# A long convolution and soft-MoE kernel: high rows' product ahead of the folds and the low rows' product in odd steps, once the last stage runs

## The chip, the cores and the metric

The kernel runs on one core of one Trainium2 chip. The metric is the time of the program on the device in microseconds; lower is better. TensorE (PE) multiplies, with its weight loads listed apart as PEld; VectorE (DVE), ScalarE (ACT) and GpSimd (POOL) compute on vectors; SyncE (SP) issues nearly all DMAs here, in one queue, in order. Each engine works through its own instructions in order and waits for the others by semaphores.

## What is computed

A long causal convolution of each of 8 sequences of 5696 tokens by 128 channels with one filter, by Fourier transform, and then a soft mixture of experts over all 45568 tokens:

```python
Xf = np.fft.rfft(x, n=L, axis=1)          # L = 2 * S
Hf = np.fft.rfft(h, n=L, axis=0)
y = np.fft.irfft(Xf * Hf[None], n=L, axis=1)[:, :S, :]
...
logits = x @ phi                          # x: y as (45568, 128); 32 slots
d = softmax of logits over all tokens     # by column
slot_input = d.T @ x
slot_out[e] = np.maximum(slot_input[e] @ w1[e], 0) @ w2[e]
c = softmax of logits over the slots      # by row
out = c @ slot_out
```

All is float32.

## The kernel before

**The transform.** The length is split into 90 x 64, so each transform is a chain of small products with a change of layout between them, for which the data goes through DRAM. Four stages follow each other, in a pipeline over *steps* t. One step brings in one tile of one sequence: 8 tiles (`NJ`) make a sequence, and the filter counts as one more sequence, ahead of the eight; so there are 72 steps (`NA`) with new input.

- *First stage*, steps 0 to 71. `load_x` (L184) brings tile t + 3 into one of three buffers `xc`, by two DMAs. `fold` (L201) adds and subtracts the two mirrored halves of a tile on GpSimd, one operation each (L206), into the four buffers `xf`, two for even tiles and two for odd ones. `first_stage` (L210) multiplies folds by the table `s1` (L217), evicts both results through ScalarE (L220) into one of four staging tiles `fst`, and stores them by SP into the DRAM tensor f of the sequence (L226). The product is made in two widths. `first_low(t)` makes rows 0 to 59 of the two folds of tile t, with weights of 128 x 64; `first_high(t)`, in odd steps alone, makes rows 60 to 89 of the four folds of tiles t - 1 and t at once, with weights of 128 x 32 side by side. Either fills two PSUM banks. Low stores two DMAs of 240 KB, high four of 120 KB.
- *Middle stage*, from step 9 on. `prefetch` loads tiles `gt` from f (L253), into four buffers. `stage_b1` (L258) multiplies them (L267, 64 x 64), VectorE applies the filter's spectrum (L285, L294). `stage_b2` (L298) multiplies back (L309, 64 x 64), ScalarE evicts (L315), and SP stores to the DRAM tensor z (L318). Odd steps have one such unit, even steps two; twelve make a sequence.
- *Last stage*, from step 27 on (`LAG_C`), over pairs of tiles. `load_pair` (L338) loads `zc` by five DMAs (L346) in even steps; there is one such buffer. `stage_c1` (L352) makes four products (L365, 128 x 64) in odd steps, in two halves, with `stage_c4` of an earlier pair between them. Its VectorE and GpSimd work gives the tokens (L370 to L384). `stage_c2` transposes (L393), `stage_c3` makes the logits (L402, 128 x 32, the last product of an even step), `stage_c4` and `stage_c5` transpose them (L431, L454), `softmax`, `dispatch` (L480) and `stage_c6` (L506) do the mixture's two softmaxes.
- After step 80 a tail without new input, and then the experts and the output.

**The order of work** is written by hand. Each step runs through a string of letters, and each letter calls one part; instructions reach every engine's queue in that order, and nothing reorders them but what an engine does itself. For odd steps it is `"xXYf1wb5s"`, for even ones `"zPxXfb26db3m"`: `x` loads a tile, `X` is `first_low`, `Y` is `first_high`, `f` folds tile t + 1, `1` is the two halves of c1 with c4 between, `w` the rest of c1's vector work, `b` a unit of the middle stage, `5` and `s` are c5 and softmax, `z` is `load_pair`, `P` is `prefetch`.

The folds of tile t + 1 go into the buffers of tile t - 1. These are read for the last time by `first_high(t)`, so in an odd step the folds wait for its products. PSUM gives the stages a ring of four banks (`bank`, L173): each use waits for the eviction of the one four uses before.

Of the kernel before, what the change touches and what calls it, by code (L numbers as in the profile page):

```python
# [12 lines left out]
AL = mybir.AluOpType  # L13
# [64 lines left out]
def kernel(  # L78
# [24 lines left out]
    nc = tc.nc  # L103
# [3 lines left out]
    E, _, F = moe_w1.shape  # L107
# [16 lines left out]
    QP = HP // 2  # L124
# [18 lines left out]
    NT = B * NQ  # L143
# [34 lines left out]
    xs = {}  # L178
    xf = [apool.tile([P, CH, D], F32, name=f"x{i}", tag=f"x{i}", bufs=1) for i in range(4)]
# [16 lines left out]
                out=t_[X0 + r.start:X0 + r.stop, :, :, :].rearrange("p s n d -> p s (n d)"), in_=v)  # L196
        xs[c] = t_

    folded = {}

    def fold(c, comp):  # L201
        if c not in xs:
            return
        t_ = xs.pop(c) if comp else xs[c]
        y_ = xf[c % 2 * 2 + comp]
        nc.gpsimd.tensor_tensor(out=y_[:, :, :], in0=t_[:, 0, :, :], in1=t_[:, 1, ::-1, :],  # L206
                                op=AL.subtract if comp else AL.add)
        folded[(c, comp)] = y_

    def first_stage(tiles, width):  # L210

        st = apool.tile([P, CH, 2, D], F32, name="fst", tag="fst", bufs=4)
        for G in range(2):
            p = bank()
            for o, (c, comp) in enumerate(tiles):
                k = slice(0, HP) if width == HP else slice(HP, HP + QP)
                nc.tensor.matmul(p[o * width:(o + 1) * width, :], s1[:, comp + G, k],  # L217
                                 folded[(c, comp)][:, :, :].rearrange("p n d -> p (n d)"),
                                 start=True, stop=True)
            nc.scalar.activation(st[:, :, G, :],  # L220
                                 p[:, :].rearrange("p (n d) -> p n d", d=D), AF.Copy)
        for o, (c, comp) in enumerate(tiles):
            g, j = divmod(c, NJ)
            n0 = comp * HALF + CH * j
            k0, n = (0, N1A) if width == HP else (N1A, N1 - N1A)
            nc.sync.dma_start(  # L226
                out=fd[g].rearrange("q a r c d -> (q a) (r c d)")[k0:k0 + n, n0 * 2 * D:(n0 + CH) * 2 * D],
                in_=st[o * width:o * width + n, :, :, :].rearrange("k n c d -> k (n c d)"))
# [2 lines left out]
        first_stage([(c, comp) for comp in range(2)], HP)  # L231

    def first_high(c):

        both = [(c - 1 + i, comp) for i in range(2) for comp in range(2)]
        first_stage(both, QP)
        for b_ in both:
            del folded[b_]

    gs, prods = {}, {}  # L240

# [82 lines left out]
    zs, ys, Ls, ds = {}, {}, {}, {}  # L324
# [5 lines left out]
    om, op = [ypool.tile([P, CH, D], F32, name=n) for n in ("om", "op")]  # L330
# [18 lines left out]
                                    a=2)[r:r + n, j * w_:(j + 1) * w_])  # L349
        zs[T] = t_  # L350

    def stage_c1(T, between):  # L352
        t_ = zs.pop(T)
        kr = used if t_ is zn else P
        y_ = ybufs.pop(0)
        ybufs.append(y_)

        def part(v, f):
            k = (2 * v + f) * CH
            return y_[:, k:k + CH, 0:D] if f == 0 else y_[:, k + CH - 1:k - 1:-1, 0:D]  # L360

        def product(o, tab, q):
            p = bank()
            for h_ in range(2):
                nc.tensor.matmul(p[h_ * HP:(h_ + 1) * HP, :], i1[0:kr, tab, :],  # L365
                                 t_[0:kr, h_, o, :, q, :], start=True, stop=True)
            return p[:, :].rearrange("p (n d) -> p n d", d=D)

        def fold_out(even, minus, plus):
            nc.vector.tensor_tensor(out=plus, in0=even, in1=minus, op=AL.add)  # L370
            nc.vector.tensor_tensor(out=minus, in0=even, in1=minus, op=AL.subtract)

        b_, a_ = product(0, 1, 1), product(0, 0, 0)
        nc.scalar.activation(part(0, 0), b_, AF.Copy)
        fold_out(a_, part(0, 0), part(1, 0))
        between()
        b_, a_ = product(1, 1, 0), product(1, 2, 1)
        nc.scalar.activation(om[:, :, :], b_, AF.Copy)

        def after():  # L380
            fold_out(a_, om[:, :, :], op[:, :, :])
            for v, o_, eng in ((1, op, nc.gpsimd), (0, om, nc.vector if tail else nc.gpsimd)):
                for part_, sign in ((part(v, 1), AL.subtract), (part(v, 0), AL.add)):
                    eng.tensor_tensor(out=part_, in0=part(v, 0), in1=o_[:, :, :], op=sign)  # L384

        ys[T] = y_
        return after

    def stage_c2(T):
        for k in (3, 1, 0, 2) if tail else (3, 2, 1, 0):  # L390
# [149 lines left out]
    LAG_B, LAG_C = NJ + 1, 3 * NJ + 3  # L540
# [24 lines left out]
    for comp in range(2):  # L565
        fold(0, comp)
    wait_b2 = []
    ORDER_E, ORDER_O, XAHEAD = "xXYf1wb5s", "zPxXfb26db3m", 3

    for t in range(last_front + 1):  # L570
        us = list(units(t))

        def pair(lag):
            T, half = divmod(t - LAG_C - lag, 2)
            return T if half == 0 and 0 <= T < NT else None

        def prefetch(last):
            nonlocal loaded
            while loaded < len(queue) and queue[loaded][1] <= last:
                load_g(queue[loaded][0])  # L580
                loaded += 1

        def slot_b():
            fresh = bool(us)
            if fresh:
                u = us.pop(0)
                stage_b1(u, t < LAG_C or t >= NA)
                wait_b2.append(u)
            if len(wait_b2) > fresh:
                stage_b2(wait_b2.pop(0))  # L590

        T, U = pair(0), pair(2)
        after = []
        work_ = {
            "z": lambda: load_pair(pair(-1)) if pair(-1) is not None else None,
            "x": lambda: load_x(t + XAHEAD) if t < NA else None,
            "p": lambda: prefetch(t + 1) if t % NJ else None,
            "P": lambda: prefetch(t + 2),
            "q": lambda: prefetch(t + 1),
            "X": lambda: first_low(t) if t < NA else None,  # L600
            "Y": lambda: first_high(t) if t < NA and t % 2 else None,
            "f": lambda: [fold(t + 1, comp) for comp in range(2)] if t < NA else None,
            "d": lambda: dispatch(pair(3)) if pair(3) is not None else None,
            "b": lambda: slot_b(),
            "1": lambda: after.append(stage_c1(T, lambda: stage_c4(U) if U is not None else None))
            if T is not None else stage_c4(U) if U is not None else None,
            "w": lambda: [a_() for a_ in after],
            "2": lambda: stage_c2(pair(1)) if pair(1) is not None else None,
            "6": lambda: stage_c6(pair(5)) if pair(5) is not None else None,
            "5": lambda: stage_c5(U) if U is not None else None,  # L610
            "3": lambda: stage_c3(pair(1)) if pair(1) is not None else None,
            "m": lambda: column_max(pair(1)) if pair(1) is not None else None,
            "s": lambda: list(softmax(U)) if U is not None else None,
            "g": lambda: prefetch(t + 1) if t % NJ == 0 else None,
        }
        if t == last_front:
            if pair(-1) is not None:
                load_pair(pair(-1))
            assert T is None and U is None
            V = pair(1)  # L620
            assert (V - 2) % NQ == 0
            slot_b()
            stage_c2(V)
            slot_b()
            dispatch(V - 1)
            stage_c3(V)
            slot_b()
            column_max(V)
            assert not us and not wait_b2
            break  # L630
        for c_ in (ORDER_E if t % 2 else ORDER_O):
            work_[c_]()
        assert not us
        if t == NA:
            lead.close()
            wts = inner.enter_context(tc.tile_pool(name="wts", bufs=1, side="right"))
            w1s = wts.tile([P, E, F], F32, name="w1s")
        if NA < t <= NA + E:
            nc.sync.dma_start(out=w1s[:, t - NA - 1, :], in_=moe_w1[t - NA - 1])
# [3 lines left out]
    T = V + 1  # L643
# [18 lines left out]
    tail["pool"] = cload.enter_context(tc.tile_pool(name="cload", bufs=1))  # L662
    y_ = tail["pool"].tile([P, Q * CH, D + 1], F32, name="y2", tag="y2", bufs=1)

    after = stage_c1(T, lambda: stage_c4(V))
    after()
    stage_c5(V)
    list(softmax(V))
    nc.gpsimd.memset(y_[:, :, D:D + 1], 1.0)
# [6 lines left out]
    for V in range(T, NT):  # L676
# [8 lines left out]
        N = T + 1 if V == T else V + 2  # L685
        after = None
        if N < NT:
            after = stage_c1(N, lambda: stage_c4(V))
            load_pair(N + 2)
        else:  # L690
            stage_c4(V)
        if after:
            after()
        stage_c5(V)
        end = softmax(V)
        if V == NT - 1:
# [6 lines left out]
            list(end)  # L703
        if V == T:
            ybufs.insert(0, y_)
            stage_c1(T + 2, lambda: None)()
            load_pair(T + 4)
        else:
            for b in range(2 * (V - T - 1), min(2 * (V - T), B - 2)):
# [4 lines left out]
                    out=w2s[:, i:i + 2, :, :],  # L714
                    in_=moe_w2[i:i + 2].rearrange("e (p c) d -> p e c d", p=P))
    stage_c6(NT - 2)
    assert list(Ls) == [NT - 1] and not (ys or ds or prods or gs or zs or xs or folded or wait_b2)


    cload.close()  # L720
# [128 lines left out]
```

## Time and profile before

| | |
|---|---|
| Time, median of 3 runs | 864.3 us (862.36 to 867.85) |
| Time of the profiled execution | 866.8 us |
| Its span, first to last instruction | 864.8 us |
| TensorE clock granted, mean | 0.943 |
| DMA, mean over the span | 315 GB/s, 272.00 MB |
| Queue of SP, share of 16 DMA engines | 90.2% |

In the table of groups, a row names the line, the engine, the operation, what is written and read with its shape, and the count; then the busy time and the mean in ns of one; then the idle time of the engine just before these instructions, and what ended most of it. A row of the waits gives who waited for whom, the total in us, the number of times and the longest one. Steps 27 to 71, in which the order changes, lie between some 170 and 626 us of the span.

### The profile page before, as it was taken

How to read it: one execution, taken by the hardware profiler on the slowest of the kernel's cores; microseconds unless marked ns; L12 is line 12 of the kernel's file. 1: busy time of each engine (PE TensorE's matmuls, PEld its weight loads, DVE VectorE, ACT ScalarE, POOL GpSimd, SP SyncE). 2: the span in 40 equal slices, each digit the busy share in tenths (PEclk: the TensorE clock that was granted, in tenths of full speed). 3: DMA queues.
4: the chain of work that ended last, by engine and by line, in shares of the span. 5: the costliest groups of instructions: out<-in, count | busy, mean ns of one | idle time of the engine just before them, and what ended most of it. 6: DMA issues, size and time to landing. Idle time of an engine off the chain costs nothing.

```text
span 864.8 us, 20506 instructions
## 1 busy us (share of the span) xinstructions
PE 777.0 (90%) x7796; PEld 376.9 (44%) x7796; DVE 618.1 (71%) x929; ACT 437.7 (51%) x967; POOL 392.6 (45%) x372
## 2 busy tenths in 40 slices
PE   5888888788999999999999999999987888978882
PEld 1122333234444444444444444444444454445882
DVE  3058877666877878887888788777879886963542
ACT  2432344344656565665566566655644445562531
POOL 4453424245556556665566555556434332541000
PEclk9999999999999999999999999999999889997755
DMA  9888999999999999999999999999987887760998
GB/s 297 265 284 300 317 328 339 336 335 342 329 316 343 341 345 324 346 334 338 322 336 348 329 342 334 344 326 345 349 298 269 285 306 261 273 267 7 370 381 328
DMA packets 153244, 272.00 MB, mean 315 GB/s; under 512 B 11878, under 2 KB 110054, under 8 KB 150005
## 3 DMA queue, kind: packets, MB, share of 16 engines
q1 hardware_dynamic: 152571, 270.38, 90.2%
q8 instruction: 62, 1.02, 0.5%
q10 hardware_dynamic: 576, 0.31, 0.1%
q14 instruction: 35, 0.29, 0.1%
HBM read 142.57 MB, written 127.98 MB: 313 GB/s over the span
## 4 chain that ended last, share of the span: by engine, by line
PE 65%; DVE 13%; DMA 8%; issue 4%; POOL 2%; ACT 1%; SPq 1%; DVEq 0%; ACTq 0%; POOLq 0%
PE bank L217 17%; PE bank L365 13%; PE bank L309 8%; PE bt L267 8%; PE bank L393 6%; DMA out_dram<-o 5%; PE bank L480 3%; DVE p L285 3%; DVE bt L285 3%; DVE yf L294 3%; PE bank L402 2%; DMA zc<-z 2%; PE bank L431 2%; POOL x L206 1%; PE bank L454 1%
## 5 line engine op out<-in xcount | busy, mean ns | idle before, releaser
L206 POOL TENSOR_TENSOR x<-xc 128x512 f32<-128x512 f32 x144 | 180.1, 1274 | 229.6 <-PE bank L217 209.2
L217 PE MATMUL bank<-x,s 128*32 128x512 f32 (+1 forms) x1152 | 229.5, 611 | 17.5 <-POOL x L206 15.8
L315 ACT ACTIVATE zst<-bank 128x512 f32<-128x512 f32 (+1 forms) x184 | 98.6, 585 | 182.2 <-PE bank L309 166.7
L220 ACT ACTIVATE fst<-bank 128x512 f32<-128x512 f32 x216 | 127.5, 598 | 110.7 <-PE bank L217 95.9
L285 DVE TENSOR_TENSOR p<-bt,Hi 128x1024 f32<-128x1024 f32 x96 | 111.3, 1159 | 34.1 <-PE bt L267 33.3
L365 PE MATMUL bank<-zc,i 128*64 128x512 f32 x480 | 118.1, 614 | 8.5 <-DMA f<-fst 5.0
L217 PEld LDWEIGHTS bank<-x,s 128*32 128x32 f32 (+1 forms) x1152 | 55.9, 124 | 158.8 <-issue 74.9
L309 PE MATMUL bank<-yf,vt 64*64 64x256 f32 x1440 | 101.6, 389 | 26.0 <-DVE yf L294 25.8
L294 DVE TENSOR_TENSOR yf<-bt,p 128x512 f32<-128x512 f32 x192 | 119.3, 663 | 3.3
L267 PE MATMUL bt<-gt,wt 64*64 64x256 f32 x1620 | 113.5, 388 | 3.7 <-DMA gt<-f 2.8
L285 DVE TENSOR_TENSOR bt<-bt,Hr 128x1024 f32<-128x1024 f32 x96 | 113.0, 1177 | 0.0
L267 PEld LDWEIGHTS bt<-gt,wt 64*64 64x64 f32 x1620 | 54.0, 132 | 78.2 <-issue 35.3
L384 POOL TENSOR_TENSOR y<-y,op 128x512 f32<-128x512 f32 x64 | 77.9, 1217 | 9.8 <-DVE op L370 6.7
L309 PEld LDWEIGHTS bank<-yf,vt 64*64 64x64 f32 x1440 | 56.6, 135 | 57.0 <-issue 28.9
L370 DVE TENSOR_TENSOR y<-bank,y 128x512 f32<-128x512 f32 x32 | 22.1, 692 | 72.5 <-PE bank L365 69.5
L393 PE MATMUL bank<-ident,y 109*128 109x109 f32 x512 | 63.9, 276 | 1.3 <-DVE y L384 1.0
L384 POOL TENSOR_TENSOR y<-y,om 128x512 f32<-128x512 f32 x54 | 64.0, 1184 | 2.1
L365 PEld LDWEIGHTS bank<-zc,i 128*64 128x64 f32 x480 | 30.4, 137 | 71.9 <-issue 47.5
L393 PEld LDWEIGHTS bank<-ident,y 109*128 109x128 f32 x512 | 53.5, 149 | 17.8 <-issue 11.5
L395 ACT ACTIVATE yt<-bank 128x360 f32<-128x360 f32 x128 | 51.3, 492 | 3.2 <-PE bank L393 3.0
L802 PE MATMUL op<-so,cT 32*128 32x128 f32 x704 | 46.2, 380 | 5.5 <-ACT o L811 5.0
L285 DVE TENSOR_TENSOR p<-bt,turn 128x1024 f32<-128x1024 f32 (+1 forms) x12 | 14.2, 1179 | 47.5 <-PE bt L267 46.7
(95 smaller groups left out, 802.0 us busy)
## 6 DMA issues: line engine op xcount, KB each, us to landing
gt<-f SPq DMA_DIRECT2D x99, 512.0 KB
z<-zst SPq DMA_DIRECT2D x88, 512.0 KB
f<-fst SPq DMA_DIRECT2D x144, 240.0 KB
zc<-z SPq DMA_DIRECT2D x30, 1024.0 KB
xc<-in_x_dram SPq DMA_DIRECT2D x64, 320.0 KB
f<-fst SPq DMA_DIRECT2D x144, 120.0 KB
out_dram<-o SPq DMA_DIRECT2D x16, 1024.0 KB
zc<-z SPq DMA_DIRECT2D x90, 128.0 KB
```

Of the source, the lines that this page charges most:

```text
L206: nc.gpsimd.tensor_tensor(out=y_[:, :, :], in0=t_[:, 0, :, :], in1=t_[:, 1, ::-1, :], op=AL.subtract if comp else AL.add)
L217: nc.tensor.matmul(p[o * width:(o + 1) * width, :], s1[:, comp + G, k], folded[(c, comp)][:, :, :].rearrange("p n d -> p (n d)"), start=Tr ...
L220: nc.scalar.activation(st[:, :, G, :], p[:, :].rearrange("p (n d) -> p n d", d=D), AF.Copy)
L267: nc.tensor.matmul(bt[q * HP:(q + 1) * HP, a, o, :], wt[r, 2 * i + q, :], t_[r, 2 * o + q, :, :].rearrange("p c d -> p (c d)"), start=True ...
L285: nc.vector.tensor_tensor(out=p_, in0=pv, in1=h_, op=AL.mult)
L294: eng.tensor_tensor(out=y_[r, 0:k, c, :], in0=pv[:, :, c, :], in1=pi[r, 0:k, 1 - c, :], op=op_)
L309: nc.tensor.matmul(bz[q][a * HP:(a + 1) * HP, o * 2 * D:(o + 1) * 2 * D], vt[r, i, a, :], y_[r, a * m + o, :, :].rearrange("p c d -> p (c ...
L315: nc.scalar.activation(st[:, 0:m, q, :], bz[q][:, 0:m * 2 * D].rearrange("p (o x) -> p o x", o=m), AF.Copy)
L365: nc.tensor.matmul(p[h_ * HP:(h_ + 1) * HP, :], i1[0:kr, tab, :], t_[0:kr, h_, o, :, q, :], start=True, stop=True)
L384: eng.tensor_tensor(out=part_, in0=part(v, 0), in1=o_[:, :, :], op=sign)
L393: nc.tensor.transpose(p[:, i * TR:(i + 1) * TR], ys[T][0:TR, k * CH + i, 0:D], ident[0:TR, 0:TR])
L395: nc.scalar.activation(yt[:, k * CH:(k + 1) * CH, :, :], of_tokens(p), AF.Copy)
```

## The change

In odd steps from step 27 on, `first_high(t)` goes ahead of `first_low(t)`, and the folds of tile t + 1 stand between them: the string becomes `"xYfX14jwb5s"`. Odd steps before 27 keep the sequence low, high, folds (`FILL_E`), and even steps keep theirs. c1 is now a generator of three parts, so that its second half has a letter of its own (`j`), and c4 one as well (`4`); both stand where they stood. `folded` was a dictionary and is now a function that names the same buffers. `load_pair` isn't called for a pair that is loaded already. The tail calls the generator's parts in the order it had.

```diff
-    folded = {}
+    def folded(c, comp):
+        return xf[c % 2 * 2 + comp]
...
-        nc.gpsimd.tensor_tensor(out=y_[:, :, :], in0=t_[:, 0, :, :], in1=t_[:, 1, ::-1, :],
-                                op=AL.subtract if comp else AL.add)
-        folded[(c, comp)] = y_
+        nc.gpsimd.tensor_tensor(out=folded(c, comp)[:, :, :], in0=t_[:, 0, :, :],
+                                in1=t_[:, 1, ::-1, :], op=AL.subtract if comp else AL.add)
...
-    def stage_c1(T, between):
+    def stage_c1(T):
...
-        between()
+        yield
...
         ys[T] = y_
-        return after
+        yield
+        after()
+        yield
...
-    ORDER_E, ORDER_O, XAHEAD = "xXYf1wb5s", "zPxXfb26db3m", 3
+    ORDER_E, ORDER_O, FILL_E, FILL_O, XAHEAD = "xYfX14jwb5s", "zPxXfb26db3m", "xXYf14jwb5s", "zPxXfb26db3m", 3
...
-        after = []
+        c1 = stage_c1(T) if T is not None else iter(())
         work_ = {
-            "z": lambda: load_pair(pair(-1)) if pair(-1) is not None else None,
+            "z": lambda: load_pair(pair(-1)) if pair(-1) is not None and pair(-1) not in zs else None,
...
-            "1": lambda: after.append(stage_c1(T, lambda: stage_c4(U) if U is not None else None))
-            if T is not None else stage_c4(U) if U is not None else None,
-            "w": lambda: [a_() for a_ in after],
+            "1": lambda: next(c1, None),
+            "4": lambda: stage_c4(U) if U is not None else None,
+            "j": lambda: next(c1, None),
+            "w": lambda: next(c1, None),
...
-        for c_ in (ORDER_E if t % 2 else ORDER_O):
+        full = t >= LAG_C
+        for c_ in ((ORDER_E if full else FILL_E) if t % 2 else (ORDER_O if full else FILL_O)):
             work_[c_]()
```

More of the change, by code (lines that the diff above doesn't have):

```diff
@@ L204, in fold @@
         t_ = xs.pop(c) if comp else xs[c]
-        y_ = xf[c % 2 * 2 + comp]
-        nc.gpsimd.tensor_tensor(out=y_[:, :, :], in0=t_[:, 0, :, :], in1=t_[:, 1, ::-1, :],
-                                op=AL.subtract if comp else AL.add)
-        folded[(c, comp)] = y_
+        nc.gpsimd.tensor_tensor(out=folded(c, comp)[:, :, :], in0=t_[:, 0, :, :],
+                                in1=t_[:, 1, ::-1, :], op=AL.subtract if comp else AL.add)
     def first_stage(tiles, width):
@@ L217, in first_stage @@
                 nc.tensor.matmul(p[o * width:(o + 1) * width, :], s1[:, comp + G, k],
-                                 folded[(c, comp)][:, :, :].rearrange("p n d -> p (n d)"),
+                                 folded(c, comp)[:, :, :].rearrange("p n d -> p (n d)"),
                                  start=True, stop=True)
@@ L233, in first_high @@
     def first_high(c):
[L235 to L238, printed above, removed]
+        first_stage([(c - 1 + i, comp) for i in range(2) for comp in range(2)], QP)
     gs, prods = {}, {}
@@ L616 @@
         if t == last_front:
-            if pair(-1) is not None:
+            if pair(-1) is not None and pair(-1) not in zs:
                 load_pair(pair(-1))
@@ L663 @@
     y_ = tail["pool"].tile([P, Q * CH, D + 1], F32, name="y2", tag="y2", bufs=1)
-    after = stage_c1(T, lambda: stage_c4(V))
-    after()
+    after = stage_c1(T)
+    next(after)
+    stage_c4(V)
+    next(after)
+    next(after)
     stage_c5(V)
@@ L687 @@
         if N < NT:
-            after = stage_c1(N, lambda: stage_c4(V))
+            after = stage_c1(N)
+            next(after)
+            stage_c4(V)
+            next(after)
             load_pair(N + 2)
@@ L692 @@
         if after:
-            after()
+            next(after)
         stage_c5(V)
@@ L705 @@
             ybufs.insert(0, y_)
-            stage_c1(T + 2, lambda: None)()
+            for _ in stage_c1(T + 2):
+                pass
             load_pair(T + 4)
@@ L716 @@
     stage_c6(NT - 2)
-    assert list(Ls) == [NT - 1] and not (ys or ds or prods or gs or zs or xs or folded or wait_b2)
+    assert list(Ls) == [NT - 1] and not (ys or ds or prods or gs or zs or xs or wait_b2)
     cload.close()
```

## The prediction

> **What bounds the kernel now.** I read the page first: engines, slices, groups.
>
> ```profile
> PE 777.0 (90%) x7796; PEld 376.9 (44%) x7796; DVE 618.1 (71%) x929; ACT 437.7 (51%) x967; POOL 392.6 (45%) x372
> ...
> L206 POOL TENSOR_TENSOR x<-xc 128x512 f32<-128x512 f32 x144 | 180.1, 1274 | 229.6 <-PE bank L217 209.2
> L217 PE MATMUL bank<-x,s 128*32 128x512 f32 (+1 forms) x1152 | 229.5, 611 | 17.5 <-POOL x L206 15.8
> ```
>
> The top group tempts: the folds wait 209.2 us for the products that the change reorders. But GpSimd is busy for 45% only, and TensorE waits for a fold for 15.8 us in all. So I asked for TensorE's waits in the stage that changes, 180 to 630 us, the whole answer but its head:
>
> ```profile
> PE bank L365 <- DMA f<-fst: 2.3, 1, 2.3
> PE bank L309 <- DVE yf L294: 2.2, 6, 0.5
> PE bank L365 <- ACT fst L220: 0.8, 1, 0.8
> PE bank L365 <- DMA zc<-z: 0.5, 2, 0.3
> ```
>
> No fold is there. Those 15.8 us lie in the fill, which keeps its order. The table of windows, one step pair (odd and even step, 20.25 us) per row; columns: stretch, us, busy us of PE, PEld, DVE, ACT, POOL, granted clock, DMA share, GB/s:
>
> ```profile
> 340.50:360.75 20.25, 20.25 (x214) 9.45 (x212) 16.61 (x25) 12.27 (x29) 11.87 (x12) 1.00 0.98 344
> 360.75:381.00 20.25, 20.25 (x214) 9.50 (x212) 16.61 (x25) 12.27 (x29) 11.88 (x12) 1.00 0.96 326
> 381.00:401.25 20.25, 19.48 (x200) 9.07 (x198) 15.08 (x25) 12.39 (x29) 12.29 (x12) 1.00 0.98 346
> 401.25:421.50 20.25, 19.90 (x202) 9.18 (x200) 16.61 (x25) 11.26 (x27) 11.02 (x12) 1.00 0.93 319
> ```
>
> TensorE is full at full clock, and so, nearly, are the transfers: the mean share of the twenty such rows from 219 to 624 us is 0.972. Two limits lie on each other. But TensorE's ends are modelled, so I looked at starts: the timeline of weight loads in one odd step (start, us, instruction, idle before).
>
> ```profile
> 417.51 0.20 PEld L217 LDWEIGHTS bank<-x,s 128*64 128x64 f32 x4 [0.59 <-issue]
> 418.00 0.14 PEld L217 LDWEIGHTS bank<-x,s 128*64 128x64 f32 x2 [0.29 <-ACT zst L315]
> 418.43 0.14 PEld L217 LDWEIGHTS bank<-x,s 128*64 128x64 f32 x2 [0.28 <-issue]
> 419.38 0.16 PEld L217 LDWEIGHTS bank<-x,s 128*32 128x32 f32 x8 [0.81 <-ACT fst L220]
> 419.84 0.13 PEld L217 LDWEIGHTS bank<-x,s 128*32 128x32 f32 x4 [0.30 <-issue]
> 420.27 0.13 PEld L217 LDWEIGHTS bank<-x,s 128*32 128x32 f32 x4 [0.30 <-issue]
> 421.24 0.20 PEld L365 LDWEIGHTS bank<-zc,i 128*64 128x64 f32 x4 [0.84 <-ACT fst L220]
> ```
>
> Passes of 512 columns start 0.43 us apart (418.00 to 418.43, 419.84 to 420.27). Where the shape of the weights changes, the loads stand idle for 0.81 to 0.84 instead of 0.3. The low product's four passes and the change to the 32-wide shape take 419.38 - 417.51 = 1.87, the high product's 421.24 - 419.38 = 1.86, against 4 x 0.43 = 1.72: a change of shape costs about **0.15 us** of TensorE inside time that the page calls busy. Lastly the queue of SP around 475 us, and the chain of waits there:
>
> ```profile
> 467.86 4.25 SPq L226 DMA_DIRECT2D f<-fst  x6
> 472.61 0.38 SPq L318 DMA_DIRECT2D z<-zst  x1
> 473.09 3.33 SPq L346 DMA_DIRECT2D zc<-z  x5
> 476.47 1.80 SPq L253 DMA_DIRECT2D gt<-f  x3
> ```
> ```profile
> 475.86 5.95 DMA zc<-z
> ```
>
> The zc load's last issue ends at 476.42 and L365 starts at 481.94: landing takes 5.5 us. With that, zc landed 1.5 us before its use at 219 us, about 0.5 us before it at 340 and 380, and too late at 400.98, 481.94 and 562.78.
>
> **What the Trainium skill says.** "TensorEngine Tiling (Array Packing)", Tiling Modes, Key Properties: changing the tiling mode, not just the tile, drains the engine. It has no price; the trace agrees with the rule. In the timeline, L267 to L309 (both 64x64) goes on at its 0.22 us pace (426.26, 426.48), and every change of shape near it costs 0.1 or more. "TensorE: Matmul & The Clock Gate", Part 2: loads are pulled ahead of running matmuls; the trace shows it within a shape and not across one. "SBUF — State Buffer", two separate sides: a GpSimd operation and a VectorE operation with two SBUF inputs lock each other out. The trace shows no such cost: folds take 1258 to 1297 ns, also in even steps where L285 and L294 run beside them. "DMA: Bandwidth & Descriptors", Specifications: about 358 GB/s of HBM per core; the fullest of the twenty rows has 349, so there is some room, not much.
>
> **The change part by part.**
> *Shapes.* From step 27 on an odd step issued, after L402 (128x32): low (128x64), high (128x32), L365 (128x64), three changes. Now: high (same shape as L402), low (a change), L365 (same shape as low). Two changes go: 2 x 0.15 = 0.30 us per odd step. Steps 27 to 71 are 23 odd ones; in 27 no L402 stands before (one change goes), and in 27 and 29 L365 waits 2.64 and 2.34 us for zc anyway, which absorbs it. Left: 21 x 0.30 = **6.3 us** at most. The price of one change is bounded by 0.09 (0.52 between starts at 418.86 and 419.38, less 0.43) and 0.18 (high product to L365: 0.12, and 0.05 in the next pass), so 3.8 to 7.6 us.
> *Folds.* The fold of step t+1 waits for the high product's last read. That ends 1.86 us sooner, 22 times. GpSimd idles 6.0 us before it (126.1 us over 21), and after it waits for L442 until 425.01 in any case: the idle time moves from before to behind. TensorE next reads these folds at 428.04, and they are done at 423.87. Worth nothing; were this cover gone, 22 x 1.86 = 41 us would be at stake. The L206 reads free xc sooner, but SP issues the load into it some 15 us later: nothing. L413 on VectorE gets a fold beside it; a full lock would hold 1.04 us back where L437 leaves 3.2 us (421.08 to 424.29): nothing.
> *Evictions.* ScalarE gets four L220 evictions in either order, 0.60 each; the four-bank ring sees the same two-and-two. Nothing.
> *DMAs.* The six f stores keep their place in SP's queue between xc and z, as four of 120 KB, then two of 240 KB, instead of the reverse. SP starts them at 426.95, when all are evicted (422.05). Sum and bytes are the same. But low rows are now the last to be issued, and six times (steps 32 to 72, where a group begins) the next gt load needs them. Behind SP's wait there: xc, f and z transfers, then the next zc. Cost between 0 and 0.9 us each: landing 5.5 against the 4.6 us from the last f issue to gt (431.24 to 435.84). I take 0.2: 1.2 us.
> The generators, the c4 slot and the `folded` function leave the order elsewhere as it was: nothing, bounds included.
>
> *Sum.* TensorE offers 6.3. The transfers must follow: same bytes in less time. At a share of 0.99 in place of 0.972, 405 us shrink by 7.4 us; at 0.98 by 3.3. I take the second, capped by the 6.3: SP's queue is also held by TensorE (the gt loads wait for L267 and L309, 10.3 us in the stage), so it gains some. **About 3.3 us less**, the 1.2 included. The profiled execution took 866.8 us (span 864.8 and 2.0 around it), 2.5 above the median 864.3: it would be 863.5, and the median **861.0**.
>
> **Rivals.** *Nothing arrives* (TensorE's gain turns into waiting at L365 for zc): for it, the late landings three times since 400 us; against it, shares of 1.00 in some rows. 864.3, give or take 1.5. *All arrives*: 858 to 859; against it the same landings. *The fold is on the path*: 864.3 - 41 = 823; against it, the four waits above. I give it 1%. *Slower*: the low stores, issued last, hold SP at the gt load of each group's head and the zc behind it; six times 0.9 and no gain gives 869.7; it decides over the gain once SP stands longer than about 1 us each time (6.3 / 6). Against it: some 5 us of queued transfers lie behind, so the engines don't run dry. *The change doesn't do what it says*: if the weights of L365 still can't be pulled ahead, for a wait on zc or a bank, only one change of shape goes: 862 to 863.
>
> **How the numbers follow.** Part of the gain, 859.5 to 863.3: 0.55. Nothing, 863.3 to 866: 0.22. All, below 859.5: 0.10. Slower, 866 and up: 0.13, of which 0.05 over 1%. The 1% (8.6 us) is about what a measurement of this kernel can tell from no change: its three runs span 5.5 us. Over 1% faster needs more than both changes of shape give: 0.04. Within: 0.91. The range 857.5 to 866.5 leaves out the slow case's most and the tip of the fast one.
>
> **What would show it.** Right: 128x32 loads behind L402 without the 0.6 idle; L365 about 3.6 us, not 3.72, after the first product, and that some 0.1 sooner after L402, where zc is there in time; the fold's wait near 4.1 us and L439's longer by 1.9; more L365 waits on zc; DMA share above 0.972. Wrong: starts across equal shapes still 0.52 apart; a pair period of 20.26 unchanged with no new zc wait; or waits of L253 on f of a microsecond and more.

## The result, and the profile after

| | before | after |
|---|---|---|
| Median of the runs | 863.3 us (859.1 to 867.9) | 874.5 us (871.3 to 876.5) |
| Profiled execution | 866.8 us | 874.9 us |
| Its span | 864.8 us | 873.1 us |

The ratio after to before is 1.0111 (95% interval 1.0069 to 1.0154). The change made the kernel slower by about 1.1%; the forecast was 861.0, and 874.5 lies above its range.

The page of after, engines and groups (`first_stage`'s product is now L216, its store L225, the product of c1 L360, the load of gt L248):

```profile
PE 770.5 (88%) x7796; PEld 381.2 (44%) x7796; DVE 643.5 (74%) x929; ACT 437.6 (50%) x967; POOL 393.1 (45%) x372
...
L206 POOL TENSOR_TENSOR x<-xc 128x512 f32<-128x512 f32 x144 | 180.2, 1275 | 184.5 <-PE bank L216 164.9
L216 PE MATMUL bank<-x,s 128*32 128x512 f32 (+1 forms) x1152 | 225.9, 610 | 16.1 <-POOL x L206 15.8
...
L360 PE MATMUL bank<-zc,i 128*64 128x512 f32 x480 | 118.2, 615 | 21.8 <-DMA zc<-z 13.6
```

TensorE does the same 7796 products in 6.5 us less busy time, and its share falls from 90% to 88% all the same. L216 still waits for folds for 15.8 us, as before: the folds are where the prediction put them. New is L360. Before, its row (then L365) read

```profile
L365 PE MATMUL bank<-zc,i 128*64 128x512 f32 x480 | 118.1, 614 | 8.5 <-DMA f<-fst 5.0
```

Its idle time was 8.5 us, most of it for f, and is 21.8 now, most of it for zc. TensorE's waits of after in the stage that changed, 180 to 630 us:

```profile
PE bank L360 <- DMA zc<-z: 10.4, 8, 2.2
PE bank L360 <- DMA xc<-in_x_dram: 2.4, 1, 2.4
PE bank L304 <- DVE yf L289: 2.2, 6, 0.5
PE bank L360 <- DMA f<-fst: 2.1, 2, 1.2
PE bank L360 <- ACT fst L219: 1.4, 2, 0.7
```

Waiting for zc was 0.5 us in two places and is 10.4 in eight. These are the late landings that the prediction saw three times; now they hold c1 in eight of the 22 step pairs. Windows of after, one step pair per row, columns as before:

```profile
338.38:358.63 20.25, 20.25 (x220) 9.77 (x216) 17.91 (x26) 12.56 (x30) 11.90 (x11) 1.00 0.98 318
358.63:378.88 20.25, 19.10 (x204) 9.22 (x196) 16.52 (x25) 11.47 (x27) 11.92 (x11) 1.00 0.99 327
378.88:399.13 20.25, 17.83 (x171) 8.07 (x167) 15.91 (x23) 11.66 (x25) 10.87 (x11) 1.00 0.94 321
399.13:419.38 20.25, 19.53 (x204) 9.14 (x197) 17.30 (x26) 11.96 (x30) 12.02 (x12) 1.00 1.00 343
```

The last two columns are the ones to read together. The DMA share is as high as before, 0.94 to 1.00, but the rate beside it is lower: 318 GB/s at a share of 0.98 where a row of before had 344 at 0.98. The same two columns over the whole stage, 200 to 620 us, first of before, then of after:

```profile
200.00:620.00 420.00, 416.97 (x4300) 194.66 (x4300) 337.88 (x519) 251.32 (x572) 247.04 (x229) 1.00 0.97 336
```
```profile
200.00:620.00 420.00, 402.75 (x4164) 191.60 (x4164) 354.30 (x507) 245.56 (x557) 241.20 (x224) 1.00 0.97 328
```

The share stays at 0.97, the rate falls from 336 to 328 GB/s, by 2.4%. TensorE stands idle for 17.3 us instead of 3.0. Those 14.2 us more, less the 6 or so that its work became shorter, give the 8.3 us by which the span grew.

Was the work on TensorE shortened as foreseen? The timeline of weight loads of after in one odd step:

```profile
338.38 0.13 PEld L216 LDWEIGHTS bank<-x,s 128*32 128x32 f32 x4 [0.17 <-issue]
338.81 0.13 PEld L216 LDWEIGHTS bank<-x,s 128*32 128x32 f32 x4 [0.30 <-ACT zst L310]
...
340.20 0.20 PEld L216 LDWEIGHTS bank<-x,s 128*64 128x64 f32 x4 [0.84 <-ACT fst L219]
340.69 0.14 PEld L216 LDWEIGHTS bank<-x,s 128*64 128x64 f32 x2 [0.28 <-issue]
341.12 0.14 PEld L216 LDWEIGHTS bank<-x,s 128*64 128x64 f32 x2 [0.28 <-issue]
341.55 0.14 PEld L360 LDWEIGHTS bank<-zc,i 128*64 128x64 f32 x2 [0.29 <-issue]
```

One gap of 0.84 is left, at 340.20, where the weights go from 32 to 64 wide. L360's weights now follow L216's after 0.29, at the pace of equal shapes. So that step works.

Where does it get lost? The start of c1's first product, after less before, over the stage: -0.45 us at the first pair (177 us), -1.4 at 259, then +0.7 at 280, +2.4 at about 320, +5.5 at 386, +7.3 at 489, +9.8 at 573, +9.0 at 633. For five pairs the change gains, about as TensorE's saving would have it. Then it goes in jumps: of the 22 intervals from pair to pair nine are 0.6 to 2.3 us longer than before, 12.4 us in sum, and ten are 0.2 to 0.9 us shorter, most by the 0.2 to 0.3 of TensorE's saving. So the saving does arrive in many pairs, and waits at c1 in the others, most of them for zc, take more than that away. One such loss in SP's timeline of after (start, duration, what is issued, count):

```profile
264.74 4.29 SPq L225 DMA_DIRECT2D f<-fst  x6
269.57 0.39 SPq L313 DMA_DIRECT2D z<-zst  x1
270.05 4.41 SPq L341 DMA_DIRECT2D zc<-z  x5
274.51 2.47 SPq L248 DMA_DIRECT2D gt<-f  x3
277.51 1.09 SPq L195 DMA_DIRECT2D xc<-in_x_dram  x2
```

and in the chain of waits of after:

```profile
273.90 6.14 DMA zc<-z
280.04 0.14 issue
280.18 1.94 PE bank L360 x8
```

The five zc issues took SP 3.33 us in the place that the prediction showed; here they take 4.41, since SP has to wait within them, and zc is 2.2 us late for L360. gt follows zc's last issue by 0.05 us: it waits for no store into f.

### The profile page after: what moved, and what is told of

Same layout as the page of the kernel before. It is cut to its first block, busy times and chain, and to the rows that moved or that the text cites. A ratio compares the mean times of both kernels' runs of the same rounds, so it can differ in the third digit from the quotient of the medians.

```text
span 873.1 us, 20484 instructions
## 1 busy us (share of the span) xinstructions
PE 770.5 (88%) x7796; PEld 381.2 (44%) x7796; DVE 643.5 (74%) x929; ACT 437.6 (50%) x967; POOL 393.1 (45%) x372
## 4 chain that ended last, share of the span: by engine, by line
PE 56%; DMA 19%; DVE 12%; SPq 3%; issue 3%; ACT 1%; POOL 1%; DVEq 0%; ACTq 0%; POOLq 0%
PE bank L360 13%; PE bank L216 12%; DMA zc<-z 9%; PE bank L304 7%; PE bt L262 7%; PE bank L390 5%; DMA out_dram<-o 5%; DMA xc<-in_x_dram 3%; SPq L341 3%; DVE yf L289 3%; PE bank L477 2%; DVE p L280 2%; DVE bt L280 2%; PE bank L428 2%; DMA gt<-f 2%
## 5 line engine op out<-in xcount | busy, mean ns | idle before, releaser
L216 PE MATMUL bank<-x,s 128*32 128x512 f32 (+1 forms) x1152 | 225.9, 610 | 16.1 <-POOL x L206 15.8
L360 PE MATMUL bank<-zc,i 128*64 128x512 f32 x480 | 118.2, 615 | 21.8 <-DMA zc<-z 13.6
L216 PEld LDWEIGHTS bank<-x,s 128*32 128x32 f32 (+1 forms) x1152 | 59.0, 125 | 149.1 <-issue 70.0
L436 POOL MEMSET dt<- 64x8 f32 x32 | 3.4, 107 | 145.2 <-ACT dn L439 77.2
L360 PEld LDWEIGHTS bank<-zc,i 128*64 128x64 f32 x480 | 32.3, 138 | 82.8 <-issue 58.8
L365 DVE TENSOR_TENSOR y<-bank,y 128x512 f32<-128x512 f32 x32 | 22.1, 692 | 57.6 <-PE bank L360 53.4
L390 PEld LDWEIGHTS bank<-ident,y 109*128 109x128 f32 x512 | 52.4, 147 | 17.2 <-issue 10.4
```

The lines of the kernel that those rows point to most:

```text
L390: nc.tensor.transpose(p[:, i * TR:(i + 1) * TR], ys[T][0:TR, k * CH + i, 0:D], ident[0:TR, 0:TR])
```

## The experiments

The change moves three things at once: TensorE's order, the folds, and the order of the six f stores in SP's queue, which follows TensorE's. My theory, after the traces: the stores' order alone costs the time, by slowing the transfers. The rivals: the folds, which now start earlier, TensorE's new order itself, and the rest of the edit, generators and so on. The first four kernels take these apart. In e1 and e2 the stores have letters of their own (`k` low, `l` high), so that the queue's order no longer follows TensorE's. The cuts of code below show the line that decides; where it has new letters, `first_stage` was also split so that its stores can be called apart.

**e0: the edit with the old order string.**

```diff
-    ORDER_E ... = "xYfX14jwb5s"
+    ORDER_E ... = "xXYf14jwb5s"
```

> The changed kernel with the old letters in odd steps (low, high, folds); all else of the change stays. Every theory of the order expects the time of the kernel before, 863 us, within 3. Over 870 would put the loss into the rest of the edit.

Measured: 864.7 us, ratio 1.0008 (0.998 to 1.0035). So the rest of the edit falls: generators and the function cost nothing that shows.

**e1: new order on TensorE, stores in the old order** (low, then high).

```diff
-    ORDER_E ... = "xYfX14jwb5s"
+    ORDER_E ... = "xYfXkl14jwb5s"
```

> The changed kernel (high product, folds, low product), but SP stores the low rows before the high ones in odd steps, as before. Theory S (the order of the f stores in SP's queue makes the transfers slower): the loss is gone and TensorE's 0.3 us per odd step begin to count, 857 to 863 us. Theory F (the earlier folds do the harm) and theory P (TensorE's faster pace itself does, by collisions of what it triggers): 874 us.

Measured: 865.6 us, ratio 1.0006 (0.9981 to 1.003). The loss is gone, with TensorE's new order in place. But in sum the gain of the shapes isn't there either. The starts of c1 say why: nine of the 22 intervals are shorter than before by 0.16 us or more, and eight are longer by 0.65 to 2.4 us.

**e2: old order on TensorE, stores in the new order** (high, then low).

```diff
-    ORDER_E ... = "xYfX14jwb5s"
+    ORDER_E ... = "xXYflk14jwb5s"
```

> The order of work of the kernel before (low, high, folds), but SP stores the high rows first in odd steps. Theory S: as slow as the change or slower, 872 to 878 us, since TensorE's gain is missing. Theories F and P: 863 us.

Measured: 872.6 us, ratio 1.0081 (1.0051 to 1.011). Turning six stores round makes the loss, with TensorE's order and the folds as they were before. Here too it comes in jumps: twelve intervals between starts of c1 are as before within 0.05 us, and eight are longer by 0.5 to 3.0. The windows of e1 and e2, 200 to 620 us:

```profile
200.00:620.00 420.00, 407.68 (x4180) 193.15 (x4176) 356.09 (x508) 247.44 (x560) 242.35 (x225) 1.00 0.97 332
```
```profile
200.00:620.00 420.00, 407.75 (x4148) 188.21 (x4147) 327.10 (x504) 245.02 (x555) 238.77 (x222) 0.99 0.97 327
```

With the new store order 327 GB/s (e2) and 328 (after), with the old one 332 (e1) and 336 (before), all at a share of 0.97. These are rates of one execution each. As the bytes are the same, a longer time is a lower rate in any case; what the row adds is that the share doesn't fall with it.

**e3: the folds held back.** As after, but the folds start only after the low product, because GpSimd first writes zeros over a corner of the table that this product reads.

```diff
+    def hold(t):
+        if t % 2 and LAG_C <= t < NA - 1:
+            nc.gpsimd.memset(s1[0:1, :, 0:1], 0.0)
...
-    ORDER_E ... = "xYfX14jwb5s"
+    ORDER_E ... = "xYXf14jwb5s"
```

> The changed kernel with the folds held until the low product has been read (a memset of three zeros into an unused row of s1 stands ahead of them on GpSimd). Theory F: the loss is gone, 857 to 863 us. Theories S and P: 874 us. If the folds are worth nothing, as the prediction had it, this differs from the change by less than 2 us.

Measured: 872.4 us, ratio 1.0088 (1.0061 to 1.0116). The zeros (L211) do hold GpSimd, 180 to 630 us:

```profile
POOL s L211 <- PE bank L220: 117.6, 20, 6.3
```

That is 5.9 us each time, as long as the folds waited before the change, and the kernel is still slow. The folds fall, and the stores' order stands.

Why should an order of equal bytes matter? SP's waits, 200 to 620 us, have rows that no data explains. First of before, then after, e1 and e2 (in the last two the store of f is L228):

```profile
SPq L195 <- DMA zc<-z: 23.5, 24, 2.5
SPq L226 <- DMA z<-zst: 19.6, 27, 1.7
```
```profile
SPq L195 <- DMA zc<-z: 28.7, 28, 3.5
SPq L225 <- DMA z<-zst: 27.7, 33, 1.1
```
```profile
SPq L195 <- DMA zc<-z: 22.5, 22, 2.4
SPq L228 <- DMA z<-zst: 18.6, 29, 1.1
```
```profile
SPq L195 <- DMA zc<-z: 24.5, 26, 2.0
SPq L228 <- DMA z<-zst: 28.6, 34, 1.0
```

A load into xc (L195) needs nothing of zc, and a store of f nothing of z. The list of waits of the program shows why SP stands (after; number, line, operation, semaphores waited for):

```
266 L225 DMACopy f_3<-fst_1845 30x1024 [waits DMAHW5_49,Activation_49]
270 L225 DMACopy f_3<-fst_1864 60x1024 [waits DMAHW1_49,Activation_49]
273 L341 DMACopy zc_110<-z_0 64x4096 [waits DMAHW4_49,PE_49]
281 L195 DMACopy xc2_104<-in_x_dram 80x2x512 [waits DMAHW4_49,Pool_49]
```

In this program there are eight semaphores for these DMAs, DMAHW0 to 7, and the DMAs take them in turn: each waits until the one eight before it has landed. Number 281 waits for 273, the zc transfer of 1024 KB. The Trainium skill, "DMA: Bandwidth & Descriptors", Anatomy of one DMA — SWDGE (gpsimd) path, says that DMA engines don't wait on semaphores, and that such a wait happens on the issuing sequencer before dispatch. The traces agree for DMAs that SP issues: it is SP that stands, for 22.5 to 28.7 us at L195, with all that is behind it. So what is under way at any time is the last eight transfers at most, whatever their size.

This gives a ruler: the time from zc's first issue to the xc load that needs zc landed. I worked its mean out from the issue starts of 15 ordinary step pairs in each timeline: 6.46 us in before, 6.69 in e1; 7.09 in after, 6.83 in e2, 6.85 in e3. It is a coarse one: single pairs of one kernel run from 5.1 to 7.8 us (before), so that a mean of 15 is uncertain by some 0.2 (my estimate from this scatter), and e1 and e2 aren't apart by it. The completion events in the traces separate them better. From issue to landing, zc's three transfers of 128 KB took 6.0 us on average in before and 6.2 in e1, against 6.7 in after, e2 and e3 (some 60 transfers each, 200 to 620 us). In these five kernels zc lands later when the high rows are stored first.

**r1 and r2: which end of the six stores matters?** One low store at each end, and two high ones at each end (A and B store one low each, C and D two high each).

```diff
-    ORDER_E ... = "xYfX14jwb5s"
+    ORDER_E ... = "xYfXACDB14jwb5s"     # r1
+    ORDER_E ... = "xYfXCABD14jwb5s"     # r2
```

> The changed kernel's order of work, with the six f stores of an odd step in the order low, high x4, low. It asks which end of the batch matters. Theory 'last' (a 240 KB store directly ahead of the z store and the zc load makes zc late): slow, 871 to 875 us. Theory 'first' (small stores directly behind the xc load let SP's queue run low): fast, 863 to 867 us, as with both low ones first (865.6).

> The same with two high stores, both low ones, two high ones. Theory 'last': fast, 863 to 867 us. Theory 'first': slow, 871 to 875 us. If neither end but the whole order counts, this and the run low, high x4, low both lie between, near 869 us.

Measured: 877.1 us, ratio 1.0167 (1.0115 to 1.0218), and 875.6, 1.0142 (1.0107 to 1.0178). Both are as slow as after. Neither "a large one must go first" nor "a small one must go last" holds: of four orders only low, low and then four high is quick. Nor do the two lie in between, near 869 us. The ruler says 6.92 and 6.81. zc's transfers of 128 KB took 6.7 us in r1 but 6.2 in r2, as in the quick e1, so their landing alone doesn't account for r2.

**r3: the zc load ahead of the stores**, at the end of the odd step (`Z` loads the next pair).

```diff
-    ORDER_E ... = "xYfX14jwb5s"
+    ORDER_E ... = "xYfX14jwbZkl5s"
```

> The changed kernel's order of work, with the zc load of the next pair issued at the end of the odd step, ahead of the six f stores (low first) instead of behind them. If late zc loads are all that keeps TensorE from its saved 0.3 us per odd step, zc now lands 3 us and more ahead of its use: 857 to 861 us. If the transfers as a whole are the bound, something else becomes late in its place (gt or the staging tiles) and the time stays at 863 to 867 us. At six group heads gt then waits for the f stores just issued, up to 5 us each: 870 us and more if that is not covered.

Measured: 880.4 us, ratio 1.0197 (1.0168 to 1.0226). That is the third of the outcomes named, 870 us and more. zc is there in time, but the waits have moved: SP's waits of this kernel, 200 to 620 us,

```profile
SPq L230 <- DMA zc<-z: 36.9, 30, 3.3
...
SPq L346 <- DMA z<-zst: 23.7, 30, 1.9
...
SPq L253 <- DMA f<-fst: 7.5, 7, 1.6
```

show the stores of f (L230) standing for zc, the zc loads (L346) for z, and the loads of gt (L253) for f, which was the foreseen part. TensorE waits for gt in turn, and longer for the middle stage's eviction into its staging tile:

```profile
PE bank L395 <- ACT zst L315: 9.9, 6, 2.3
PE bt L267 <- DMA gt<-f: 6.0, 10, 0.8
```

**t1 and t2: stores of one size.** The low stores of odd steps are cut into halves of 30 rows, so that eight stores of 120 KB take the place of two and four. t1 has the low ones first, t2 last.

```diff
+            for i in range(0, n, cut or n):
+                m = min(cut or n, n - i)
...
-    ORDER_E ... = "xYfX14jwb5s"
+    ORDER_E ... = "xYfXKl14jwb5s"       # t1: K is the low stores in halves
+    ORDER_E ... = "xYfXlK14jwb5s"       # t2
```

> The changed kernel's order of work, f stores low rows first, but each low store of an odd step in two halves of 30 rows: eight stores of 120 KB each, two transfers more in a step pair. Theory 'place' (the low rows' writes must not stand near the z store and zc load, because of where in DRAM they go): about the 865.6 us of the unsplit run, plus what two transfers cost. Theory 'size' (a 240 KB store among the last four makes zc late): the same here, so this run is the base of the next.

> The same eight stores of 120 KB, with the high rows' four ahead and the low rows' four behind. Theory 'place': 8 to 10 us slower than with the low rows first, as unsplit. Theory 'size': within 3 us of it, since every store has the same size wherever it stands.

Measured: 888.6 us, ratio 1.0301 (1.0253 to 1.0348), and 887.4, 1.0291 (1.0233 to 1.0349). With equal sizes the order makes no difference at this level. As both are slower than after, the runs don't tell whether equal sizes take the effect away or a larger loss covers it. Two more transfers per step pair with the same bytes go with 23 us more than e1. That they also shift which transfers are eight apart, and that a half has 30 rows instead of 60, isn't separated here. The ruler reads 6.67 and 6.69, as in e1: it doesn't see this loss.

**t3: wider rows of f.** Each q of f is padded from 128 to 132 KB, high stores first, to see whether the place that a store writes to matters.

```diff
-    fd = ... (NP, 2 * N2, 2, D)
+    fd = ... (NP, 2 * N2 + 4, 2, D)
```

> The changed kernel as it is (high rows stored first), with the DRAM tensor f laid out so that two rows lie 132 KB apart instead of 128 KB: the same transfers with other addresses. Theory 'place': the time changes by several us, to 868 or below if the rows' common pitch is what collides. Theories 'size' and 'eight in flight': 874 us, within 2.

Measured: 908.6 us, ratio 1.0553 (1.0468 to 1.0638). No theory foresaw that. The stores' access pattern had to change with the padding, so it is no clean test of place, and it stays unexplained.

**t4: zc in one transfer** of 90 rows instead of five, low stores first; the tail's copy of rows held over is left out with it.

```diff
+    return [(0, n, 0, 1)]               # z_blocks: one block
```

> High product, folds, low product with the low rows stored first (865.6 us), and the zc load of a pair as one transfer of 90 rows on consecutive partitions instead of five of 64, 8, 8, 8 and 2 rows. Theory 'eight in flight' (SP starts a transfer only when the one eight before it has landed, so small transfers starve the queue): 19 instead of 23 transfers in a step pair carry the same bytes, zc lands a microsecond or more sooner, and TensorE's 0.3 us per odd step count at last: 856 to 861 us. If the number of transfers doesn't matter: 864 to 867 us.

Measured: 936.6 us, ratio 1.0845 (1.079 to 1.0901), the opposite of what fewer transfers should give. Its windows, 200 to 620 us, and SP's waits there:

```profile
200.00:620.00 420.00, 376.93 (x3736) 175.05 (x3726) 318.29 (x456) 222.24 (x501) 216.38 (x200) 0.96 0.98 297
```
```profile
SPq L317 <- DMA zc<-z: 47.2, 19, 4.3
```

The rate is 297 GB/s at a share of 0.98, and SP stands for zc at the z store, which is now the eighth behind it. From its issue the one transfer lands after some 10.7 us. Where c1 waits for zc, e1's five take 7.0 to 10.0 us from their first issue to the last landing. The run changes the number, the layout on the partitions and who is eight behind whom all at once, so it is no test of the number alone.

**v0, v1 and v2: one load fewer per tile.** The two loads of xc become one of 96 rows for most sequences; that leaves 21 transfers in a step pair rather than 23. v0 is before with it, v1 is e1 with it, v2 is after with it.

```diff
-        for r in (slice(0, SPLIT), slice(SPLIT, R1)):
+        rows = (slice(0, SPLIT), slice(SPLIT, R1))
+        if 0 < g < B:
+            src = x[g - 1:g + 1].rearrange("b (a n) d -> (b a) n d", n=N2)
+            rows = (slice(0, SPLIT + 16),)
+        for r in rows:
```

> The kernel before with the wider xc loads. TensorE keeps its three changes of shape in an odd step, so it can gain only the waits for zc in the stage (some 3 us) and what the fill gains: 857 to 862 us. The run with the new order of work and the low rows stored first should be 3 to 6 us faster than this one, TensorE's 0.3 us on 20 odd steps, if the shapes are worth what the starts in the trace say.

> High product, folds, low product with the low rows stored first (865.6 us), and each xc load of sequences 1 to 7 as one transfer of 96 rows (the last 7 belong to the next sequence and meet zeros in s1) instead of two of 80 and 9: 21 transfers in a step pair instead of 23, with 56 KB more. Theory 'eight in flight': the two halved runs paid some 23 us for two transfers more, so two fewer free SP's queue, zc is in time, and TensorE becomes the bound with its saved 0.3 us: 855 to 861 us. If the number of transfers doesn't count by itself: 864 to 868 us.

> The changed kernel as it is (high rows stored first, 874 us) with the same wider xc loads. Theory 'eight in flight': the order of the f stores cost time only because the queue held too few bytes; with two transfers fewer it costs less than 3 us against the run with the low rows first. If the order costs by itself (the sizes next to the zc load): still 8 to 10 us slower than that run.

Measured: ratios 0.9977 (0.9952 to 1.0003), 0.9974 (0.9943 to 1.0006) and 0.9968 (0.9946 to 0.999). The gains foreseen for v0 and v1 didn't come, nor did the 3 to 6 us between them; v1's runs spread widely, from 856.3 to 876.9 us. v2, at 862.7 us, is after in all but this load, and the 1.1% are gone, high stores first or not; the ruler reads 6.48. It beats both kernels, before by 0.3%, but stands no lower than v0 within the intervals. So another entry of SP's queue, the load of xc that stands just ahead of the stores in an odd step and again in the even one, decides whether their order costs anything. That two transfers less aren't worth 23 us, as two more cost in t1, says that the number alone isn't the measure.

**n0 and n1: transfers taken off the bound.** The loads of xc for tiles 30 to 71 are left out, in before (n0) and in after (n1); the folds work on what the buffers hold.

```diff
         xs[c] = t_
+        if c >= 30:
+            return
```

> The kernel before without the xc loads of tiles 30 to 71: the folds work on what the buffers hold, so the output isn't the reference's, and 712 KB in a step pair are missing from the transfers. TensorE is then the only bound in the stage: about 3 us of waits go, 857 to 862 us, and the tail may gain a little more.

> The changed kernel without the same xc loads. If a change of shape costs TensorE 0.15 us, 20 to 23 odd steps with two fewer make this 6 to 7 us faster than the kernel before without the loads. If the pace of starts in the trace misled and the shapes are free, within 1.5 us of it. If the order of the f stores still costs, slower than it.

Measured: 854.8 us, ratio 0.9895 (0.9861 to 0.9928), and 848.9, ratio 0.9812 (0.9749 to 0.9876). With room for the transfers, the change makes the kernel faster, by 5.8 us between the medians and 6.1 between the spans (858.5 and 852.4). n1 has only four runs, but its trace says the same: c1 starts 20.26 us apart in n0 (260.33, 280.59) and 19.97 in n1 (255.39, 275.36), and 19 of the 22 intervals differ by this 0.29. n1 stores the high rows first, as after does, and no loss shows. The windows of n0 and n1, 200 to 600 us:

```profile
200.00:600.00 400.00, 396.85 (x4093) 184.54 (x4090) 321.91 (x494) 240.39 (x546) 235.36 (x218) 1.00 0.88 303
```
```profile
200.00:600.00 400.00, 397.78 (x4153) 190.63 (x4150) 352.50 (x504) 243.31 (x553) 240.20 (x223) 1.00 0.90 308
```

At a share of 0.88 to 0.90 TensorE is busy for over 99% in both, and neither has one wait of TensorE for zc.

## Why the prediction was wrong, by its steps

- **Shapes**: right in size. It said 0.30 us per odd step and 6.3 in all; n1 against n0 gives 0.29 per step pair and 5.8 to 6.1. In after, L360 follows the first product by 3.59 us (338.38 to 341.97), with 3.6 foreseen.
- **Folds, worth nothing**: right. e3 shows that their place doesn't cause the loss, and n1 against n0 leaves nothing over for them. The waits moved as said, GpSimd's of before and then of after, 180 to 630 us:

```profile
POOL x L206 <- PE bank L217: 126.1, 21, 6.5
POOL dt L439 <- ACT dn L442: 24.3, 20, 2.0
```
```profile
POOL x L206 <- PE bank L216: 83.9, 21, 4.5
POOL dt L436 <- ACT dn L439: 75.3, 20, 5.5
```

The fold's wait went from 6.0 to 83.9 / 21 = 4.0 us (4.1 foreseen), that for the operation after it (L439, now L436) from 1.2 to 3.8 (3.1 foreseen). One reading on the way was wrong. The prediction took the folds beside L285 and L294 as a trial of the lock between GpSimd and VectorE. Both of these read `bt`, which lies in PSUM, and only one tile in SBUF, so they aren't operations with two SBUF inputs. Nothing here shows what the lock costs.
- **Evictions and the rest of the edit, nothing**: e0 agrees for the edit outside the order; no run takes the evictions alone.
- **DMAs**: this is the step that failed. "Sum and bytes are the same", it said, and the cost would be at most 0.9 us at six group heads. Sum and bytes were the same, but the transfers weren't: e2 against before is 8.8 us, a mean of 0.40 us per step pair over 22 of them, and after against e1, measured apart, is 8.9. It falls on eight or nine of the pairs. In after SP has no wait of gt (L248) on f between 180 and 630 us. The prediction priced who waits for the moved stores' data, and put at nothing what their order does to the transfers around them. The link that it didn't look at is shown: each DMA in SP's queue also waits for the landing of the one eight before it, whatever the data. That this link is how the order costs its time isn't shown.
- **"The transfers must follow"**: failed as well. It read the share of 0.97 as room, from 0.97 to 0.98. In after the share is 0.97 and the rate 2.4% lower. Even with the stores put back (e1) nothing of the 6.3 us arrived in sum. Nor is the 358 GB/s beside which the prediction set its fullest row a ceiling: near its end before moves 370 and 381 GB/s in two slices of 21.6 us, with other transfers. What holds the stage at 336 is open.
- **Rivals**: *nothing arrives* is what e1 is, TensorE's gain turned into waiting at c1 (for zc 8.2 us, 200 to 620 us). For after itself the sign was *slower*'s, but its mechanism, SP held at gt, wasn't there, and its price of 5.4 us was half of the 11.2 measured. That the bound at c1 is a late zc was read rightly, and it is the place where the loss comes out.

**What stays open.** That the order of the stores costs the time is shown (e1, e2), in this queue and not in v2's or n1's. That SP is held by the transfer eight before is shown by its waits and the program's list; that the order acts through this alone isn't. For it: the waits of f stores for z grow with the new order (19.6 and 18.6 to 27.7 and 28.6), and one load fewer elsewhere in the queue takes the effect away (v2). With equal sizes there is none either, but at a slower level (t1, t2). Against a simple form of it: counting the bytes of the last eight transfers puts the mixed orders of r1 and r2 between the two, and they were as slow as after; and in r1 the stores' waits for z came to 19.3 us only, as in before. A rival stands untested: the place in DRAM that a store writes to, for which t3 was no clean trial. Another is how each transfer is spread over the 16 DMA engines, of which the share and the rate give only the mean.

## What to carry to other kernels

Where transfers are as full as the bound engine, an edit of the bound engine's order is also an edit of the DMA queue: list the queue's order before and after, with sizes, and look in the program's waits for which transfer each one waits, data or not. Moving the stores by letters of their own, so that their order stays, separates the two at once. A mean over all pairs can hide that a gain arrives in one pair and is lost in the next: look at the starts pair by pair. And a high DMA busy share isn't throughput: read the GB/s beside it.

## What the runs showed of the hardware

- The busy share of the DMA engines was 0.97 at 336 GB/s (before), 0.97 at 328 (after) and 0.98 at 297 (t4, zc in one transfer). So it doesn't tell what they moved. It isn't fixed either: in t1, at 314 GB/s, it was 0.95. What fills the rest of the busy time isn't shown.
- A change of the weights' shape between products, here between 128x32 and 128x64 in float32, costs TensorE about 0.15 us and shows as busy time. The Trainium skill, "TensorEngine Tiling (Array Packing)", Tiling Modes, Key Properties, states the drain without a price; n1 against n0 puts 5.8 to 6.1 us on about 42 changes, 0.14 us each.
- With two stores of 240 KB per pair cut into four of 120 KB the kernel took 23 us more (t1 against e1). Joining two loads into one took the loss of 1.1% from after (v2), and did nothing clear for before (v0). Fewer and larger wasn't always better: with the one zc load of t4 the kernel took 72 us more than before.
